# A tuned convolution-and-rational-network kernel: literal biases by rescaling, one engine relieved, head reordered

## The chip, the cores and the metric

The kernel runs on one core of one Trainium2 chip. The metric is the device time of one execution in microseconds (us). The core's engines work side by side and meet through semaphores: TensorE (PE; PEld is its weight load), VectorE (DVE), ScalarE (ACT), GpSimd (POOL) and SyncE (SP), whose queue issues all the DMAs here.

## The reference

First comes a depthwise convolution over 7 steps of the sequence, with a softmax over its taps, for 8 heads of 24 channels each. Its result is the input of a network with a rational function between two products:

```python
w = softmax(weight)                              # (8 heads, 7 taps)
x = causal_conv(x, w).reshape(32768, 192)        # x: (8, 4096, 192)
h = x @ w_in                                     # (192, 2048)
P = a[0] + a[1]*h + a[2]*h**2 + a[3]*h**3
Q = 1.0 + abs(b[0])*abs(h) + abs(b[1])*h**2
out = (P / (Q + 1e-6)) @ w_out                   # (2048, 192)
```

a is drawn as four normal numbers times 0.3, b as two times 2.4. For the default seed b is 0.417 and 1.823.

## The kernel before

**Chunks and units.** The 32768 tokens are cut into 64 chunks of 512 (NCH), the 2048 hidden channels into 8 units of 256 (UPC). So there are 512 units, numbered k = 8c + i. For each chunk, `conv` (task c, two halves, 108 small matmuls) makes the convolution in PSUM; ScalarE casts it (xh, L394 and L397) and VectorE takes the residuals (xl, L404 and L408). For each unit, `gemm1` (g1, 10 matmuls, L417) makes h in one of two PSUM buffers (tile hp). Then come the passes over 128 x 1024 elements below, and `gemm2` (g2, 16 matmuls in two pairs, L426) adds g times the second weights into the one PSUM tile op. At a chunk's end `out_evac` (O, L435) scales it into ob, and SP writes it out.

**The passes of a unit on the fast path** (function `unit`), with K0, K1, K2, BETA, DD columns of the tile cf:

- S (ScalarE, L457): t = square(h + K2). A (ScalarE, L461): A = abs(r_sq h), with a scale from a register.
- B (ScalarE, L464): A = square(A + BETA). L (L471): y = ln(A + DD). Y (L473): y = exp(-y), the reciprocal of the denominator.
- V (VectorE): t = (t + K1) h. m (VectorE): g = (t + K0) y.
- e: A = (A + DD) y. In even units it is one VectorE operation; in odd units (ON_POOL) it is two on GpSimd, q (L483, the sum) and e (L486, the product).
- g (VectorE): g = (A - 2) g. This product by a value near 1 makes up for the error of y.

VectorE's V, m, e and g all come through the helper `stt` and show as L258: V writes t, e writes A, m is g<-t,cf,y and g is g<-A,g.

**The branch.** A fast path and a general path are both in the program. The flag ok, worked out on VectorE from a and b, decides at run time. The general path has a fifth VectorE pass (U) and other ScalarE arguments. Before the change, the condition on b is b0 squared / 8 <= |b1|.

**The weights.** They arrive as 64-bit floats in 16 pieces (8 of w_in, called i, and 8 of w_out, called o, in the order RAW, through 8 buffers) and are made into 32-bit ones during chunk 0, by the steps a, d (ScalarE), m (GpSimd), s, o (VectorE), r (GpSimd), and for w_in h (ScalarE, the upper part wh_t) and l (GpSimd, the lower part wl_t). Chunk 0's products wait for them.

**What sets the order.** `plan` works out one fixed order of all tasks on the engines by a list schedule: each task has an engine, a cost from the table COST (or PREP), dependences and a rank; an engine that comes free takes the ready task of the lowest rank. TensorE's own order is written by hand: g1(k), at i = 4 the next chunk's two convolution halves, then g2(k - 3). Dependences put in for buffers are that g1(k) waits for V, A and S of k - 2, and g2 of a chunk's first unit waits for the O of the chunk before. Each engine then runs its queue in that order and waits where data is late. The head (softmax of the taps, flag, coefficients, first loads) lies ahead of that, and the transfers go out on SP's queue in the order of the code.

Of the kernel before, what the change touches and what calls it, by code (L numbers as in the profile page):

```python
# [166 lines left out]
def kernel(  # L167
# [91 lines left out]

    a = [ab_t[:, i:i + 1] for i in range(6)]  # L260
    nc.scalar.activation(out=cf[:, B0:B0 + 2], in_=ab_t[:, 4:6], func=AF.Abs)
    nc.scalar.activation(out=cf[:, 18:22], in_=ab_t[:, 0:4], func=AF.Abs)
    m0, m1, m2, m3 = (col(18 + i) for i in range(4))
# [293 lines left out]
```

## Time and profile before

| | |
|---|---|
| median of 3 runs | 2833.69 us (2833.64 to 2834.93) |
| profiled execution, time | 2833.45 us |
| profiled execution, span (first to last instruction) | 2831.6 us |
| mean granted TensorE clock | 0.992 of full speed |
| busy PE / PEld / DVE / ACT / POOL | 2701.2 / 2407.0 / 2437.2 / 2757.8 / 1508.8 us |

Busy time is a sum over the span. The end is set by whichever engine others wait for in a stage, so stages are read apart: the head with chunk 0, the steady chunks, the end. Neighbouring operations of one engine overlap by some 0.1 us in their durations, so the distance between starts is what an engine's pace is read from.

### The profile page before, as it was taken

What the parts mean: (1) busy time and instruction counts of PE and PEld (TensorE: products, weight loads), DVE (VectorE), ACT (ScalarE), POOL (GpSimd) and SP (SyncE); (2) the same over time, 40 slices, a digit from 0 to 9 for tenths busy, and PEclk for the clock granted to TensorE, in tenths of its full rate; (3) what the DMA queues carried; (4) which work ended last, traced back from release to release, by engine and by line L of the source; (5) the groups of instructions that cost most, each with busy time, mean ns of one, the idle gap of its engine ahead of it and who ended that gap; (6) DMA issues with size and microseconds to landing.
All of it is one profiled execution on the core that took longest, in us unless ns stands there. A gap on an engine that the chain in (4) does not pass through costs nothing.

```text
span 2831.6 us, 49117 instructions
## 1 busy us (share of the span) xinstructions
PE 2701.2 (95%) x20224; PEld 2407.0 (85%) x20224; DVE 2437.2 (86%) x2061; ACT 2757.8 (97%) x2927; POOL 1508.8 (53%) x560
## 2 busy tenths in 40 slices
PE   5899999999999999999999999999999999999998
PEld 4788888888888888888888888888888888888887
DVE  6888888888888888888888888888888888888887
ACT  6899999999999999999999999999999999999998
POOL 7755555455554555555554545545555555545454
PEclk8999999999999999999999999999999999999999
DMA  4000000000000000000000000000000000000000
GB/s 135 13 23 14 25 19 19 25 19 19 25 16 22 25 13 25 23 14 25 18 19 25 18 19 25 16 22 25 13 25 23 15 25 18 19 25 18 19 12 13
DMA packets 49194, 64.44 MB, mean 23 GB/s; under 512 B 4672, under 2 KB 43840, under 8 KB 48960
## 3 DMA queue, kind: packets, MB, share of 16 engines
q1 hardware_dynamic: 48960, 61.22, 7.6%
q8 instruction: 160, 2.62, 0.4%
q14 instruction: 74, 0.61, 0.1%
HBM read 36.03 MB, written 25.17 MB: 22 GB/s over the span
## 4 chain that ended last, share of the span: by engine, by line
ACT 60%; issue 18%; PE 8%; POOL 8%; DVE 5%; DMA 0%; SPq 0%; DVEq 0%; POOLq 0%
ACT A L464 14%; ACT t L457 13%; ACT A L461 12%; ACT y L471 10%; ACT y L473 6%; PE hp L417 4%; POOL A L486 4%; POOL A L483 3%; PE op L426 2%; DVE g L258 2%; DVE A L258 2%; PE cps L387 2%; ACT xh L397 1%; ACT xh L394 1%; ACT ob L435 1%
## 5 line engine op out<-in xcount | busy, mean ns | idle before, releaser
L483 POOL TENSOR_SCALAR A<-A,cf 128x1024 f32<-128x1024 f32 x256 | 795.6, 3108 | 1257.8 <-ACT y L471 1257.8
L426 PE MATMUL op<-wo_t,g 128*128 128x192 f32 x8192 | 1431.2, 328 | 5.2 <-DVE g L258 4.2
L426 PEld LDWEIGHTS op<-wo_t,g 128*128 128x128 f32 x8192 | 1351.1, 190 | 63.2 <-ACT ob L435 23.9
L417 PE MATMUL hp<-xh,wh_t 128*128 128x512 f32 x2048 | 870.6, 425 | 105.4 <-DVE t L258 90.2
L258 DVE SCALAR_TENSOR_TENSOR g<-A,g 128x1024 f32<-128x1024 f32 x512 | 678.1, 1324 | 267.0 <-POOL A L486 267.0
L258 DVE SCALAR_TENSOR_TENSOR g<-t,cf,y 128x1024 f32<-128x1024 f32 x512 | 763.5, 1491 | 87.4 <-ACT y L473 87.4
L486 POOL TENSOR_TENSOR A<-A,y 128x1024 f32<-128x1024 f32 x256 | 649.9, 2539 | 34.8 <-DVE xh L408 18.7
L258 DVE SCALAR_TENSOR_TENSOR t<-t,cf,hp 128x1024 f32<-128x1024 f32 x512 | 650.7, 1271 | 0.3 <-ACT t L457 0.3
L417 PE MATMUL hp<-xh,wl_t 128*128 128x512 f32 x2048 | 639.5, 394 | 6.2 <-POOL wl_t L364 6.1
L471 ACT ACTIVATE y<-A,cf 128x1024 f32<-128x1024 f32 x512 | 588.8, 1150 | 16.4
L464 ACT ACTIVATE A<-A,cf 128x1024 f32<-128x1024 f32 x512 | 587.6, 1148 | 0.0
L457 ACT ACTIVATE t<-hp,cf 128x1024 f32<-128x1024 f32 x512 | 567.9, 1109 | 0.0
L417 PEld LDWEIGHTS hp<-xh,wh_t 128*128 128x128 f32 x2048 | 388.0, 189 | 207.6 <-DVE t L258 72.9
L473 ACT ACTIVATE y<-y 128x1024 f32<-128x1024 f32 x512 | 539.7, 1054 | 6.3
L461 ACT ACTIVATE A<-hp 128x1024 f32<-128x1024 f32 x512 | 514.9, 1006 | 1.9 <-PE hp L417 1.9
L417 PEld LDWEIGHTS hp<-xh,wl_t 128*128 128x128 f32 x2048 | 387.3, 189 | 96.1 <-POOL wl_t L364 8.9
L417 PE MATMUL hp<-xl,wh_t 128*128 128x512 f32 x1024 | 404.6, 395 | 0.0
L258 DVE SCALAR_TENSOR_TENSOR A<-A,cf,y 128x1024 f32<-128x1024 f32 x256 | 328.4, 1283 | 0.0
L417 PEld LDWEIGHTS hp<-xl,wh_t 128*128 128x128 f32 x1024 | 194.8, 190 | 20.7
L387 PEld LDWEIGHTS cps<-wb_t,xs 128*32 128x32 f32 x6912 | 117.1, 149 | 30.9 <-issue 30.9
L387 PE MATMUL cps<-wb_t,xs 128*32 128x58 f32 (+1 forms) x6912 | 125.1, 229 | 7.9 <-DVE cf L290 7.9
L435 ACT ACTIVATE ob<-op 128x384 f32<-128x384 f32 x128 | 62.3, 488 | 8.8 <-PE op L426 8.8
(46 smaller groups left out, 311.0 us busy)
## 6 DMA issues: line engine op xcount, KB each, us to landing
out<-ob SPq DMA_DIRECT2D x128, 192.0 KB, 2.0
xs<-in_xa SPq DMA_DIRECT2D x64, 324.0 KB, 3.9
xs<-in_xb SPq DMA_DIRECT2D x64, 108.0 KB, 3.7
raw<-in_w_in SPq DMA_DIRECT2D x8, 512.0 KB, 8.6
raw<-in_w_out SPq DMA_DIRECT2D x8, 384.0 KB, 7.5
wb_t<-in_wband SPq DMA_DIRECT2D x1, 174.0 KB, 2.4
mb_t<-in_mband SPq DMA_DIRECT2D x1, 174.0 KB, 2.7
wr_t<-in_wrep SPq DMA_DIRECT2D x1, 21.0 KB, 2.4
```

The lines of the kernel that those rows point to most:

```text
L258: nc.vector.scalar_tensor_tensor(out=out_, in0=a, scalar=s, in1=b, op0=op0, op1=op1)
L387: nc.tensor.matmul(cps[32 * j:32 * j + 32, blk * BW:blk * BW + n], lhsT=xs[:, :, blk, g], rhs=wb_t[:, g, 0:n], start=True, stop=True, tile ...
L417: nc.tensor.matmul(H[k][:, j, :], lhsT=w[:, i, part, j, :], rhs=x, start=(n == 0), stop=(n == 4))
L426: nc.tensor.matmul(O[c][:, t, 0:D], lhsT=G[k][:, j, t * P:t * P + P], rhs=wo_t[:, f, :], start=(f == 0 and t % 2 == 0), stop=(f == FT - 1 ...
L435: nc.scalar.activation(out=ob, in_=o, func=AF.Copy, scale=r_na3)
L457: nc.scalar.activation(out=work_tile(k, "t"), in_=h, func=AF.Square, bias=col(K2))
L461: nc.scalar.activation(out=work_tile(k, "A"), in_=h, func=AF.Abs, scale=r_sq if fast else r_b0)
L464: nc.scalar.activation(out=s["A"], in_=s["A"], func=AF.Square, bias=col(BETA))
L471: nc.scalar.activation(out=y, in_=s["A"], func=AF.Ln, bias=col(DD) if fast else C_Q)
L473: nc.scalar.activation(out=s["y"], in_=s["y"], func=AF.Exp, scale=-1.0)
L483: nc.gpsimd.tensor_scalar(s["A"], s["A"], col(DD), None, ALU.add)
L486: nc.gpsimd.tensor_tensor(out=s["A"], in0=s["A"], in1=s["y"], op=ALU.mult)
```

## The change

The fast path's formulas are rescaled so that the biases of S, B and L become the literal 1: S is square(rt h + 1), A is abs(rA h) with another scale, B is square(A + 1), L is ln(rL A + 1), where rt, rA, rL (and rO for O) are scales in ScalarE registers. VectorE's passes keep their form with new constants: V with c1, m with c0, e with d, and g with d2 = 2d from a tile where the literal 2 stood. All units do e on VectorE; GpSimd's q and e are gone, so GpSimd only prepares weights (and the general path's Q).

The coefficients are no longer worked out in the head. A new VectorE task k (43 operations on 128 x 1, then four register loads on ScalarE) does so behind chunk 0's residuals, and every S and A depends on it. The flag's condition is written anew, with b0 squared <= 3 |b1| and bounds on both, and stands behind the softmax in the code. The first weight piece is loaded ahead of chunk 0's x. The costs and arrival times of `plan` are set anew. The entry of h in the table H is deleted with g and no longer with V.

The diff, cut to its core (the general path's side and the old coefficient code are left out):

```diff
-COST = {"c": 1100, "g1": 2290, "g2": 1300, "xh": 460, "xl": 600, "S": 905, "A": 905, "B": 905, "L": 949, "Y": 958,
-        "V": 1198, "m": 1198, "e": 1200, "g": 1142, "q": 1250, "f": 2500, "O": 357, "U": 1198, "Q": 2500}
+COST = {"c": 950, "g1": 2280, "g2": 1300, "xh": 460, "xl": 600, "S": 905, "A": 905, "B": 905, "L": 949, "Y": 950,
+        "V": 1195, "m": 1196, "e": 1196, "g": 1142, "k": 6000, "O": 357, "U": 1198, "Q": 2500}
...
-ON_POOL = (1, 3, 5, 7)
...
-    arrive, last = 9000, {}
+    arrive, last = 5500, {}
     for n, (which, i) in enumerate(RAW):
-        arrive += 2600 if which == "i" else 2000
+        arrive += (2600 if which == "i" else 2000) + (2200 if n in (1, 3) else 0)
...
-            add(("c", c, half), "PE", COST["c"], deps, 0, 6000 if c == 0 else 0)
+            add(("c", c, half), "PE", COST["c"], deps, 0, 9800 if c == 0 else 0)
...
+    add(("k", 0), "DVE", COST["k"], [("xl", 0, 0), ("xl", 0, 1)], -40)
...
-        add(("S", k), "ACT", COST["S"], [("g1", k)] + old(4, "m"), 8 * k + 1)
-        add(("A", k), "ACT", COST["A"], [("g1", k)] + old(4, "g"), 8 * k)
+        add(("S", k), "ACT", COST["S"], [("g1", k), ("k", 0)] + old(4, "m"), 8 * k + 1)
+        add(("A", k), "ACT", COST["A"], [("g1", k), ("k", 0)] + old(4, "g"), 8 * k)
...
-        if fast and i in ON_POOL:
-            add(("q", k), "POOL", COST["q"], [("L", k)], 8 * k + 5)
-            add(("e", k), "POOL", COST["f"], [("q", k), ("Y", k)], 8 * k + 6)
-        else:
-            add(("e", k), "DVE", COST["e"], [("Y", k)], 8 * k + 6)
+        add(("e", k), "DVE", COST["e"], [("Y", k)], 8 * k + 6)
...
+    load_w(*RAW[0])
     load_x(0)
-    for which, i in RAW[:2]:
+    for which, i in RAW[1:3]:
         load_w(which, i)
     load_x(1)
-    for which, i in RAW[2:NRAW]:
+    for which, i in RAW[3:NRAW]:
         load_w(which, i)
-
...
-    stt(col(K2), a[2], 0.5, col(R3), ALU.mult, ALU.mult)
...
-    stt(col(BETA), col(B0), 0.5, col(RQ), ALU.mult, ALU.mult)
-    stt(col(T0), col(BETA), -1.0, col(BETA), ALU.mult, ALU.mult)
-    ts(col(DD), col(T0), C_Q, None, ALU.add)
...
-    for name, i in (("r_b0", B0), ("r_sq", SQ), ("r_na3", NEG_A3)):
-        reg = nc.scalar.alloc_register(name)
-        nc.scalar.reg_load(reg, col(i)[0:1].bitcast(I32))
-        scales.append(reg)
-    r_b0, r_sq, r_na3 = scales
...
+    stt(less[:, 6:7], b0, 1.0, b0, ALU.mult, ALU.mult)
+    ts(more[:, 6:7], b1, 3.0, None, ALU.mult)
...
+    nc.vector.tensor_tensor(out=less, in0=less, in1=more, op=ALU.is_le)
+    nc.vector.tensor_reduce(out=col(24), in_=less, axis=AX.X, op=ALU.min)
+    nc.vector.tensor_copy(out=ok, in_=col(24))
...
-                nc.scalar.activation(out=ob, in_=o, func=AF.Copy, scale=r_na3)
+                nc.scalar.activation(out=ob, in_=o, func=AF.Copy, scale=K["rO"])
...
+        def coefficients():
...
+            def div(x, y):
+                r, q = spare(), spare()
+                nc.vector.reciprocal(out=r, in_=y)
+                stt(q, r, -1.0, y, ALU.mult, ALU.mult)
+                stt(r, q, 2.0, r, ALU.add, ALU.mult)
+                stt(r, x, 1.0, r, ALU.mult, ALU.mult)
+                return r
+
+            regs = {}
+            if fast:
+                regs["t"] = div(a[3], a[2])
+                ts(regs["t"], regs["t"], 2.0, None, ALU.mult)
+                K["c0"], K["c1"], K["d"], K["d2"], w, x = (spare() for _ in range(6))
+                ts(w, regs["t"], 2.0, None, ALU.mult)
+                inv = div(w, a[2])
+                stt(K["c0"], a[0], 1.0, inv, ALU.mult, ALU.mult)
+                stt(K["c1"], a[1], 1.0, inv, ALU.mult, ALU.mult)
+                ts(K["c1"], K["c1"], -1.0, None, ALU.add)
+                regs["A"] = div(b1, b0)
+                ts(regs["A"], regs["A"], 2.0, None, ALU.mult)
...
+                ts(x, b0, 0.0, 1.0, ALU.mult, ALU.add)
+                regs["L"] = div(x, K["d"])
...
+                regs["O"] = div(w, x)
...
+            for name, x in regs.items():
+                K["r" + name] = nc.scalar.alloc_register(f"r_{name}_{fast}")
+                nc.scalar.reg_load(K["r" + name], x[0:1].bitcast(I32))
...
+            if kind == "k":
+                coefficients()
+            elif kind == "S":
                 if fast:
-                    nc.scalar.activation(out=work_tile(k, "t"), in_=h, func=AF.Square, bias=col(K2))
+                    nc.scalar.activation(out=work_tile(k, "t"), in_=h, func=AF.Square, scale=K["rt"], bias=1.0)
...
             elif kind == "A":
-                nc.scalar.activation(out=work_tile(k, "A"), in_=h, func=AF.Abs, scale=r_sq if fast else r_b0)
+                nc.scalar.activation(out=work_tile(k, "A"), in_=h, func=AF.Abs, scale=K["rA"])
             elif kind == "B":
                 if fast:
-                    nc.scalar.activation(out=s["A"], in_=s["A"], func=AF.Square, bias=col(BETA))
+                    nc.scalar.activation(out=s["A"], in_=s["A"], func=AF.Square, bias=1.0)
...
             elif kind == "L":
-                y = work_tile(k, "y") if fast else s["y"]
-                nc.scalar.activation(out=y, in_=s["A"], func=AF.Ln, bias=col(DD) if fast else C_Q)
+                if fast:
+                    nc.scalar.activation(out=work_tile(k, "y"), in_=s["A"], func=AF.Ln, scale=K["rL"], bias=1.0)
...
             elif kind == "V":
-                stt(s["t"], s["t"], col(K1) if fast else na1, h, ALU.add, ALU.mult)
-                del H[k]
+                stt(s["t"], s["t"], K["c1"], h, ALU.add, ALU.mult)
             elif kind == "m":
                 G[k] = gpool.tile([P, 2, CH], F32, name="g")
-                stt(flat(G[k]), s["t"], col(K0) if fast else na0, s["y"], ALU.add, ALU.mult)
-            elif kind == "q":
-                nc.gpsimd.tensor_scalar(s["A"], s["A"], col(DD), None, ALU.add)
+                stt(flat(G[k]), s["t"], K["c0"], s["y"], ALU.add, ALU.mult)
             elif kind == "e":
-                if fast and k % UPC in ON_POOL:
-                    nc.gpsimd.tensor_tensor(out=s["A"], in0=s["A"], in1=s["y"], op=ALU.mult)
-                else:
-                    stt(s["A"], s["A"], col(DD) if fast else C_Q, s["y"], ALU.add, ALU.mult)
+                stt(s["A"], s["A"], K["d"] if fast else C_Q, s["y"], ALU.add, ALU.mult)
             elif kind == "g":
-                stt(flat(G[k]), s["A"], 2.0, flat(G[k]), ALU.subtract, ALU.mult)
-                del st[k]
+                stt(flat(G[k]), s["A"], K["d2"] if fast else 2.0, flat(G[k]), ALU.subtract, ALU.mult)
+                del st[k], H[k]
```

## Rows read from the trace of the kernel before

**Rows 1.** Engines' busy time (share of the span, instructions), and the chain of work that ended last, shares by engine.

```profile
PE 2701.2 (95%) x20224; PEld 2407.0 (85%) x20224; DVE 2437.2 (86%) x2061; ACT 2757.8 (97%) x2927; POOL 1508.8 (53%) x560
...
ACT 60%; issue 18%; PE 8%; POOL 8%; DVE 5%; DMA 0%; SPq 0%; DVEq 0%; POOLq 0%
```

**Rows 2.** The table by stretches: from:to, length, busy us of PE, PEld, DVE, ACT, POOL with counts, granted clock, DMA share, GB/s.

```profile
0.00:44.00 44.00, 15.97 (x138) 10.87 (x138) 27.98 (x68) 24.38 (x40) 30.62 (x28) 0.83 0.72 201
...
500.00:931.00 431.00, 419.02 (x3162) 374.19 (x3161) 374.96 (x311) 427.08 (x451) 225.64 (x80) 1.00 0.07 21
```

**Rows 3.** The first evacuations of chunk 0 and of chunk 62 in ScalarE's timeline (start, us, what), with, between them, the group of A passes from 114 to 2786.6 us.

```profile
114.23 0.49 ACT L435 ACTIVATE ob<-op 128x384 f32<-128x384 f32 x1
...
L461 ACT ACTIVATE A<-hp 128x1024 f32<-128x1024 f32 x496 | 498.8, 1006 | 0.0
...
2786.53 0.48 ACT L435 ACTIVATE ob<-op 128x384 f32<-128x384 f32 x1
```

**Rows 4.** Who waited for whom from 114 to 2786 us: us in total, times, longest.

```profile
PEld hp L417 <- DVE t L258: 54.9, 61, 0.9
PEld hp L417 <- issue: 53.0, 61, 1.4
PEld op L426 <- ACT ob L435: 23.6, 62, 1.2
```

**Rows 5.** ScalarE's passes, grouped from 114 to 2786.6 us (count | busy us, mean ns | idle us before); A is in group 3.

```profile
L471 ACT ACTIVATE y<-A,cf 128x1024 f32<-128x1024 f32 x496 | 570.5, 1150 | 16.1
L464 ACT ACTIVATE A<-A,cf 128x1024 f32<-128x1024 f32 x496 | 569.3, 1148 | 0.0
L457 ACT ACTIVATE t<-hp,cf 128x1024 f32<-128x1024 f32 x496 | 550.2, 1109 | 0.0
L473 ACT ACTIVATE y<-y 128x1024 f32<-128x1024 f32 x496 | 522.9, 1054 | 6.1
```

**Rows 6.** ScalarE's timeline in the steady part: S, B, L and the next A.

```profile
1397.04 1.10 ACT L457 ACTIVATE t<-hp,cf 128x1024 f32<-128x1024 f32 x1
1398.04 1.14 ACT L464 ACTIVATE A<-A,cf 128x1024 f32<-128x1024 f32 x1
1399.21 1.15 ACT L471 ACTIVATE y<-A,cf 128x1024 f32<-128x1024 f32 x1
1400.27 1.00 ACT L461 ACTIVATE A<-hp 128x1024 f32<-128x1024 f32 x1
```

**Rows 7.** TensorE's weight loads in the timeline: one unit with a convolution, then one without.

```profile
1411.66 0.19 PEld L417 LDWEIGHTS hp<-xh,wh_t 128*128 128x128 f32 x1
...
1414.22 1.80 PEld L387 LDWEIGHTS cps<-wb_t,xs 128*32 128x32 f32 x108 [0.36 <-issue]
...
1418.62 0.19 PEld L417 LDWEIGHTS hp<-xh,wh_t 128*128 128x128 f32 x1
...
1429.27 0.19 PEld L417 LDWEIGHTS hp<-xh,wh_t 128*128 128x128 f32 x1
...
1434.15 0.19 PEld L417 LDWEIGHTS hp<-xh,wh_t 128*128 128x128 f32 x1
```

**Rows 8.** VectorE's timeline in the steady part: an m beside GpSimd's q (which runs from 1395.38 for 3.87 us), then g, m, e, V, g.

```profile
1397.18 1.42 DVE L258 SCALAR_TENSOR_TENSOR g<-t,cf,y 128x1024 f32<-128x1024 f32 x1 [0.65 <-ACT y L473]
...
1401.74 1.23 DVE L258 SCALAR_TENSOR_TENSOR g<-A,g 128x1024 f32<-128x1024 f32 x1 [1.96 <-POOL A L486]
1402.88 1.28 DVE L258 SCALAR_TENSOR_TENSOR g<-t,cf,y 128x1024 f32<-128x1024 f32 x1
1404.08 1.28 DVE L258 SCALAR_TENSOR_TENSOR A<-A,cf,y 128x1024 f32<-128x1024 f32 x1
1405.28 1.27 DVE L258 SCALAR_TENSOR_TENSOR t<-t,cf,hp 128x1024 f32<-128x1024 f32 x1
1406.47 1.25 DVE L258 SCALAR_TENSOR_TENSOR g<-A,g 128x1024 f32<-128x1024 f32 x1
```

**Rows 9.** VectorE's timeline from a chunk's first residual to the g behind the last.

```profile
65.60 0.88 DVE L408 TENSOR_TENSOR xh<-cps,xh 64x290 fp32r<-64x290 f32 x2
...
67.11 1.59 DVE L258 SCALAR_TENSOR_TENSOR g<-A,g 128x1024 f32<-128x1024 f32 x1
```

**Rows 10.** VectorE's m, grouped from 500 to 931 us.

```profile
L258 DVE SCALAR_TENSOR_TENSOR g<-t,cf,y 128x1024 f32<-128x1024 f32 x80 | 119.8, 1497 | 14.0 <-ACT y L473 14.0
```

**Rows 11.** The table by stretches, the first 104 us (columns as in group 2).

```profile
0.00:104.00 104.00, 58.27 (x401) 46.73 (x402) 74.87 (x110) 68.71 (x96) 83.02 (x54) 0.80 0.33 92
```

**Rows 12.** GpSimd's q and e, grouped from 0 to 92.7 us.

```profile
L483 POOL TENSOR_SCALAR A<-A,cf 128x1024 f32<-128x1024 f32 x3 | 10.2, 3400 | 0.0
...
L486 POOL TENSOR_TENSOR A<-A,y 128x1024 f32<-128x1024 f32 x3 | 7.1, 2356 | 0.1
```

**Rows 13.** VectorE's timeline in the head: two of the coefficient operations, then the second weight piece's s step.

```profile
7.10 0.15 DVE L255 TENSOR_SCALAR cf<-cf 128x1 f32<-128x1 f32 x1
7.29 0.22 DVE L258 SCALAR_TENSOR_TENSOR cf<-cf,ab_t 128x1 f32<-128x1 f32 x1
...
17.73 1.50 DVE L352 TENSOR_SCALAR tr<-ad 128x512 uint32<-128x512 uint32 x1 [2.90 <-POOL ad L346]
```

**Rows 14.** TensorE's timeline in the head: the first product.

```profile
16.95 0.80 PE L417 MATMUL hp<-xh,wh_t 128*128 128x512 f32 x1 [6.20 <-ACT wh_t L362]
```

**Rows 15.** VectorE's timeline at the end: the last g.

```profile
2821.72 1.23 DVE L258 SCALAR_TENSOR_TENSOR g<-A,g 128x1024 f32<-128x1024 f32 x1 [2.24 <-POOL A L486]
```

More of the change, by code (lines that the diff above doesn't have):

```diff
@@ L217 @@
     sm = const.tile([P, NG], F32, name="sm")
-    cf = const.tile([P, 32], F32, name="cf")
+    cf = const.tile([P, 64], F32, name="cf")
     ok = const.tile([P, 1], I32, name="ok")
@@ L258, in stt @@
         nc.vector.scalar_tensor_tensor(out=out_, in0=a, scalar=s, in1=b, op0=op0, op1=op1)
[L260 to L263, printed above, removed]
-    ts(col(T0), m3, 2.0 ** -40, None, ALU.is_ge)
-    stt(col(T1), m2, 1.0 / 16.0, m3, ALU.mult, ALU.is_le)
-    stt(col(T0), col(T0), 1.0, col(T1), ALU.mult, ALU.mult)
@@ L448, in work_tile, with spare @@
             return t
-        na0, na1, na2, na3 = (col(NEG + i) for i in range(4))
+        K = {}
+        def coefficients():
+            def spare():
+                K["n"] = K.get("n", 24) + 1
+                return col(K["n"])
+            def div(x, y):
[17 more added lines that the diff above has]
+                ts(regs["A"], regs["A"], 2.0, None, ALU.mult)
+                ts(w, regs["A"], 2.0 * C_Q, None, ALU.mult)
+                d = div(w, b0)
+                ts(K["d"], d, -1.0, None, ALU.add)
+                ts(K["d2"], K["d"], 2.0, None, ALU.mult)
+                ts(x, b0, 0.0, 1.0, ALU.mult, ALU.add)
+                regs["L"] = div(x, K["d"])
+                ts(w, regs["A"], 2.0, None, ALU.mult)
+                beta2 = div(b0, w)
+                stt(w, K["d"], 1.0, beta2, ALU.mult, ALU.mult)
+                stt(w, w, 1.0, K["d"], ALU.mult, ALU.mult)
+                stt(x, w, -1.0, inv, ALU.mult, ALU.mult)
+                ts(w, b0, 0.0, 1.0, ALU.mult, ALU.add)
+                regs["O"] = div(w, x)
+            else:
+                K["c0"], K["c1"], K["c2"], regs["t"] = (spare() for _ in range(4))
+                for x, y in zip((K["c0"], K["c1"], K["c2"], regs["t"]), a):
+                    ts(x, y, -1.0, None, ALU.mult)
+                regs["A"] = b0
+                root, rec = spare(), spare()
+                ts(root, b1, 1e-30, None, ALU.max)
+                nc.scalar.activation(out=root, in_=root, func=AF.Ln)
+                nc.scalar.activation(out=root, in_=root, func=AF.Exp, scale=0.5)
+                nc.vector.reciprocal(out=rec, in_=root)
+                stt(root, rec, b1, root, ALU.mult, ALU.add)
+                ts(root, root, 0.5, None, ALU.mult)
+                regs["B"] = root
+            for name, x in regs.items():
+                K["r" + name] = nc.scalar.alloc_register(f"r_{name}_{fast}")
+                nc.scalar.reg_load(K["r" + name], x[0:1].bitcast(I32))
@@ L469, in unit @@
             elif kind == "L":
-                y = work_tile(k, "y") if fast else s["y"]
-                nc.scalar.activation(out=y, in_=s["A"], func=AF.Ln, bias=col(DD) if fast else C_Q)
+                if fast:
+                    nc.scalar.activation(out=work_tile(k, "y"), in_=s["A"], func=AF.Ln, scale=K["rL"], bias=1.0)
+                else:
+                    nc.scalar.activation(out=s["y"], in_=s["A"], func=AF.Ln, bias=C_Q)
             elif kind == "Y":
```

59 lines of the change are left out of this document (19 added, 40 removed).

## The prediction

> **What bounds the kernel now.** I read the page first for the engines' shares and the chain that ended last: ScalarE is busy 97% of the span, TensorE 95%, VectorE 86%, and the chain runs 60% over ScalarE [rows 1]. Such shares mix stages, so next comes the table by stretches: in the middle ScalarE is busy 427.1 of 431 us, at a granted TensorE clock of 1.00, the 2.4 GHz level [rows 2]. Then the evacuations of the output, one pair per chunk: chunk 0's first is at 114.23 us, chunk 62's at 2786.53, with 62 x 8 units of ScalarE passes between [rows 3]. A chunk takes (2786.53 - 114.23) / 62 = 43.10 us. So the time is a head of 114.2, 62 chunks of 43.10 and a rest of 2831.6 - 2786.5 = 45.1. The steady chunk is ScalarE's: it hardly idles, while TensorE's weight loads wait for VectorE's t pass (V) (54.9 + 53.0, the latter named issue) and for the output's evacuation (23.6) [rows 4], in all (54.9 + 53.0 + 23.6) / 62 = 2.1 us a chunk.
>
> **ScalarE's passes.** Three of five take a bias from the tile cf: S 1109 ns, B 1148, L 1150; two take none: A, from PSUM, 1006, Y, from SBUF, 1054 [rows 5]. The change makes these three biases the literal 1. No row has a pass with a literal bias other than zero, so its cost lies between the bias-free rows and the tile rows. I take the bias-free ones, as Y already runs with a literal scale of -1 and A with a register scale at no visible price. S is then like A, B and L like Y: (1109 - 1006) + (1148 - 1054) + (1150 - 1054) = 103 + 94 + 96 = 293 ns a unit, 2.34 us a chunk. ScalarE's chunk falls from 43.10 to 40.76, if its order stays. It can fall further: L starts 1.17 us after the B that it needs, where other neighbours start 1.00 and 1.06 apart [rows 6]; eight such joints are worth about 1 us, if the new order parts them. Bounds for ScalarE: 39.8 to 43.10.
>
> The Trainium skill has a price for this, in "ScalarE: Activation LUTs", section "What ACT_TABLE_LOAD costs": a pass with literal scale and bias has the smaller fixed cost, and each per-partition operand adds about 93 ns. By it, ScalarE's chunk would be 43.10 - 24 x 0.093 = 40.87, an estimate; the rows' 94 to 103 ns agree and go into the sum.
>
> **What is late next: TensorE.** Where nothing holds it, one unit's first weight load follows the last one's by 1434.15 - 1429.27 = 4.88 us; the unit with a convolution takes 1418.62 - 1411.66 = 6.96, of which 0.36 is a gap named issue in front of the convolution [rows 7]. A chunk is 7 x 4.88 + 6.96 = 41.12 us, more than ScalarE's 40.76. So the gain per chunk is capped near 43.10 - 41.12 = 1.98, and not 2.34.
>
> **VectorE takes four more passes.** The product e of the odd units leaves GpSimd and its q disappears; VectorE does e for all 8 units, and g gets a tile scalar (d2) for the literal 2. Neighbours start 1.20 us apart after m and after e, 1.19 after V, 1.14 after a g with the literal [rows 8]; g with a tile scalar is taken at e's 1.20. A unit is 4.79, eight are 38.3, and the two residual steps of the next chunk add 67.11 - 65.60 = 1.51 [rows 9]: 39.8 us a chunk. This hides under TensorE's 41.12 with 1.3 us to spare. The other bound: m averages 1497 ns where it runs 1.28 alone [rows 8, 10]; if that stretch stayed on m, a unit would be 5.01 and a chunk 41.6. I take the short rows, since the 1.42 us m in group 8 ran beside a GpSimd pass and the 1.28 ones did not. What is queued behind VectorE is V, which frees the PSUM buffer that TensorE wants two units later.
>
> **The steady chunk.** Floor 41.12; of the 2.1 us that TensorE waits now, some stay, since ScalarE at 40.76 and VectorE at 39.8 are both close behind and only two PSUM buffers lie between. With none left the chunk is 41.1, with all 43.1. I take 0.3 (nearer to none: the waits arise because ScalarE is slower than TensorE, which ends): 41.4, a saving of 62 x 1.7 = 105 us. The waits of VectorE for GpSimd's product (1.96 us ahead of one g, [rows 8]) go too, and are worth nothing by themselves, as VectorE isn't the bound.
>
> **The head.** GpSimd is busy 83.0 of the first 104 us [rows 11]; until the last l step, which ends at 92.7, q and e take 10.2 + 7.1 = 17.3 of it [rows 12], between the steps of the weight preparation that chunk 0 waits for. Against it stands the new step k: the coefficients, until now interleaved in VectorE's idle start, become 43 small operations behind chunk 0's residuals. Neighbours of that kind start 0.19 apart (7.10 to 7.29 us) [rows 13], so 8.2 us. Behind k on VectorE wait the s and o steps of the second weight piece, which begin at 17.73 now [rows 13]; with k from about 13 to 21 they are 3.5 late. Behind its four register loads on ScalarE wait chunk 0's S and A, which need them, and the a, d and h steps of later pieces, whose room is GpSimd's backlog. Four more e on VectorE (4.8) count by half, as VectorE idles in the head. Gain 17.3 - 3.5 - 2.4 = 11. Bounds: 17 if all of GpSimd's time comes back, a loss of 13 if nothing does and k and the four e count in full. On SP's queue the first weight piece now goes ahead of chunk 0's x, which comes later by one issue of about 0.5 us and by 512 KB at the head's mean rate of 201 GB/s [rows 2], 2.6 us: the convolution may start up to 3 us later. I cost this at nothing, since the first product waits until 16.95 for the weights, 6.2 us of it idle [rows 14]; if that cover is gone, it costs those 3. The first part of the coefficient work that stays ahead of the branch is smaller than now and costs nothing.
>
> **The rest.** At the end the last g waits 2.24 us for GpSimd's product [rows 15]; that wait goes, and the last chunk gets 1.7 shorter: 45.1 - 3.9 = 41.1.
>
> **Sum.** 103.2 + 62 x 41.4 + 41.1 = 2711.1 us of span. The profiled execution took 2833.45 against its span of 2831.6, so 1.9 lie around it; it is 0.2 under the median of the runs. Forecast: 2713 us.
>
> **The rivals.**
> (a) The waits stay. ScalarE and VectorE alternate in a fixed order, and bursts (the casts after a convolution, the evacuations) make V late, so that TensorE keeps losing over a microsecond a chunk, or m stays stretched. For it: three engines within 1.3 us of one another. Against: a unit's first product is through 1414.22 - 0.36 - 1411.66 = 2.2 us after it begins [rows 7], and its buffer is wanted two units, 9.8 us, after that beginning, which leaves over 7 us for A, S and V. At 42.3 a chunk: 103.2 + 2622.6 + 42 + 1.9 = 2770.
> (b) TensorE is quicker than I read: the 0.36 gap before the convolution goes, since ScalarE no longer delays anything. A chunk of 40.76 gives 103.2 + 2527.1 + 40.5 + 1.9 = 2673.
> (c) The change doesn't do what it says: the literal 1 costs as much as the tile did. ScalarE's chunk stays 43.1, only head and end gain: 103.2 + 2672.2 + 42.8 + 1.9 = 2820.
> (d) Slower: VectorE becomes the bound. With 32 passes a chunk and 1.51 of residuals, it passes 43.10 when passes follow one another by 1.30 us on average. If the three passes that read two SBUF tiles kept the 1497 ns of today's m (1.42 apart) and V its 1.20, a chunk would be 8 x 5.46 + 1.51 = 45.2: 103.2 + 2802 + 47 + 1.9 = 2954. For it: that mean. Against: it is seen beside GpSimd, which is idle after the head.
> The Trainium skill bears on this in "SBUF — State Buffer", section "SBUF: two separate sides": a VectorE instruction with two SBUF inputs and a GpSimd one that reads SBUF lock each other out of a shared port pair. By that rule the stretch ends with GpSimd's passes; the trace agrees as far as the m of 1.42 and 1.28 us go.
> (e) The narrower condition fails for the inputs and the general path runs: five VectorE passes a unit, 8 x 5 x 1.20 + 1.51 = 49.5 a chunk, some 3220 us. The drawn b has b0 squared over |b1| of 0.095, against an allowed 3.
>
> **How the numbers follow.** Forecast (chunks of 41.1 to 41.9, 2690 to 2745): 0.60. (a) 0.17, (b) 0.11, (c) 0.04, (d) 0.04, (e) 0.02, anything else 0.02. For 8 in 10, the range reaches into (b) and (a): 2668 to 2775; the head's bounds (6 us less to 24 more) lie within. This kernel can be told from no change by about 0.2%, 6 us. Faster: the forecast, (a), (b) and three quarters of (c) with the rest, 0.92; the same 0.02; slower, with (d) and (e), 0.06.
>
> **What would show it.** Right: S near 1006 ns, B and L near 1054; TensorE's weight loads following without waits for most of a chunk, evacuations 41 to 42 us apart; V, m, e and g all 1.2 us apart; GpSimd idle after some 85 us; chunk 0's evacuation near 103. Wrong: S, B or L unchanged; VectorE busy throughout with TensorE waiting for it over 1 us a chunk; chunk 0 later than 114, with VectorE's run of tiny operations in its chain.

## The result, and the profile of the changed kernel

The changed kernel takes 2704.05 us (median of 4 runs, 2703.7 to 2705.01) against 2833.80 before in the same comparison: a ratio of 0.9542, 95% interval 0.9525 to 0.9558. It is faster by 4.6%; the forecast was 2713 with a range of 2668 to 2775. The profiled execution took 2705.01 us, with a span of 2703.2 and a mean granted clock of 0.992, the same as before.

The page first, engines' busy time and shares of the chain that ended last, to be laid beside [rows 1]:

```profile
PE 2647.6 (98%) x20224; PEld 2412.1 (89%) x20224; DVE 2592.2 (96%) x2339; ACT 2604.8 (96%) x2924; POOL 65.3 (2%) x48
...
PE 96%; DVE 1%; POOL 1%; ACT 1%; issue 1%; DMA 0%; SPq 0%; POOLq 0%; DVEq 0%
```

The chain has gone over from ScalarE (60% before) to TensorE (96%). ScalarE is still 96% busy, so its share of busy time alone would not tell that it no longer bounds anything. The steady stretch, from the table by stretches (columns as in [rows 2]):

```profile
500.00:931.00 431.00, 431.00 (x3268) 393.71 (x3268) 418.42 (x367) 423.06 (x472) 0.00 (x0) 1.00 0.07 21
```

TensorE is busy all 431 us, and GpSimd does nothing. ScalarE's first evacuation of chunk 0 and of chunk 62, as in [rows 3]:

```profile
110.60 0.49 ACT L396 ACTIVATE ob<-op 128x384 f32<-128x384 f32 x1 [1.07 <-PE op L387]
...
2659.57 0.49 ACT L396 ACTIVATE ob<-op 128x384 f32<-128x384 f32 x1 [0.50 <-PE op L387]
```

A chunk is (2659.57 - 110.60) / 62 = 41.11 us instead of 43.10. Of the 128.4 us that the span lost, 123.3 came from the 62 steady chunks, 1.99 each. Head and rest, which were 114.2 + 45.1 = 159.3, are 110.6 + 43.6 = 154.2: another 5.1, of which 3.6 in the head and 1.5 in the rest.

Who waited for whom from 97 to 2660 us, the three largest entries (us in total, times, longest):

```profile
DVE g L249 <- ACT y L493: 73.1, 62, 1.8
ACT ob L396 <- PE op L387: 31.4, 63, 1.1
PEld cps L348 <- issue: 21.8, 62, 0.4
```

TensorE's waits for VectorE's t pass and for the evacuation [rows 4] are gone from the list. What is left of TensorE's own is the 0.35 us in front of each convolution. VectorE and ScalarE now wait once a chunk, for ScalarE and for TensorE: that is what the slack of engines that don't bound looks like. ScalarE's passes, grouped from 500 to 1793 us (count | busy us, mean ns | idle us before), against [rows 5]:

```profile
L489 ACT ACTIVATE y<-A 128x1024 f32<-128x1024 f32 x253 | 268.1, 1060 | 8.0
L482 ACT ACTIVATE A<-A 128x1024 f32<-128x1024 f32 x252 | 267.2, 1060 | 0.0
L493 ACT ACTIVATE y<-y 128x1024 f32<-128x1024 f32 x252 | 264.4, 1049 | 0.0
L475 ACT ACTIVATE t<-hp 128x1024 f32<-128x1024 f32 x252 | 256.8, 1019 | 0.0
L479 ACT ACTIVATE A<-hp 128x1024 f32<-128x1024 f32 x252 | 253.6, 1006 | 0.0
```

S fell from 1109 to 1019 ns, B from 1148 to 1060, L from 1150 to 1060: 90 + 88 + 90 = 268 ns a unit. A is as it was, and Y nearly so. VectorE, grouped from 500 to 931 us:

```profile
L249 DVE SCALAR_TENSOR_TENSOR t<-t,cf,hp 128x1024 f32<-128x1024 f32 x85 | 108.2, 1273 | 0.0
L249 DVE SCALAR_TENSOR_TENSOR g<-t,cf,y 128x1024 f32<-128x1024 f32 x84 | 107.3, 1278 | 11.7 <-ACT y L493 11.7
L249 DVE SCALAR_TENSOR_TENSOR A<-A,cf,y 128x1024 f32<-128x1024 f32 x84 | 107.3, 1278 | 0.0
L249 DVE SCALAR_TENSOR_TENSOR g<-A,cf,g 128x1024 f32<-128x1024 f32 x84 | 107.3, 1277 | 0.0
```

The m that averaged 1497 ns [rows 10] takes 1278. TensorE's pace is seen in the block loads of the output product, one unit and the next, in its timeline:

```profile
1403.63 2.69 PEld L387 LDWEIGHTS op<-wo_t,g 128*128 128x128 f32 x16
...
1408.51 2.69 PEld L387 LDWEIGHTS op<-wo_t,g 128*128 128x128 f32 x16
```

They are 4.88 us apart, what [rows 7] have for units that nothing holds; at this pace, with 6.95 us for the unit with the convolution, a chunk takes its 41.11.

### The profile page after: what moved, and what is told of

It is laid out like the page before. It is cut to its first block, busy times and chain, and to the rows that moved or that the text cites. A ratio compares the mean times of both kernels' runs of the same rounds, so it can differ in the third digit from the quotient of the medians.

```text
span 2703.2 us, 48126 instructions
## 1 busy us (share of the span) xinstructions
PE 2647.6 (98%) x20224; PEld 2412.1 (89%) x20224; DVE 2592.2 (96%) x2339; ACT 2604.8 (96%) x2924; POOL 65.3 (2%) x48
## 4 chain that ended last, share of the span: by engine, by line
PE 96%; DVE 1%; POOL 1%; ACT 1%; issue 1%; DMA 0%; SPq 0%; POOLq 0%; DVEq 0%
PE op L387 49%; PE hp L378 42%; PE cps L348 4%; POOL ad L307 0%; DVE g L249 0%; POOL tr L321 0%; DMA xs<-in_xb 0%; POOL wo_t L321 0%; DVE A L249 0%; DVE cf L249 0%; ACT A L479 0%; DVE t L249 0%; ACT A L482 0%; ACT y L493 0%; ACT t L475 0%
## 5 line engine op out<-in xcount | busy, mean ns | idle before, releaser
L249 DVE SCALAR_TENSOR_TENSOR g<-t,cf,y 128x1024 f32<-128x1024 f32 x512 | 655.4, 1280 | 74.3 <-ACT y L493 74.3
L249 DVE SCALAR_TENSOR_TENSOR A<-A,cf,y 128x1024 f32<-128x1024 f32 x512 | 658.9, 1287 | 0.0
L249 DVE SCALAR_TENSOR_TENSOR g<-A,cf,g 128x1024 f32<-128x1024 f32 x512 | 654.9, 1279 | 0.0
L489 ACT ACTIVATE y<-A 128x1024 f32<-128x1024 f32 x512 | 542.5, 1060 | 16.0
L482 ACT ACTIVATE A<-A 128x1024 f32<-128x1024 f32 x512 | 542.9, 1060 | 0.0
L475 ACT ACTIVATE t<-hp 128x1024 f32<-128x1024 f32 x512 | 521.7, 1019 | 0.0
L479 ACT ACTIVATE A<-hp 128x1024 f32<-128x1024 f32 x512 | 515.3, 1006 | 0.8 <-PE hp L378 0.8
L369 DVE TENSOR_TENSOR xh<-cps,xh 64x290 fp32r<-64x290 f32 (+1 forms) x128 | 54.0, 422 | 3.7
L358 ACT CAST xh<-cps 64x290 fp32r<-64x290 f32 (+1 forms) x128 | 46.2, 361 | 3.5 <-PE cps L348 2.7
```

The costliest lines, as they stand in the source:

```text
L249: nc.vector.scalar_tensor_tensor(out=out_, in0=a, scalar=s, in1=b, op0=op0, op1=op1)
L358: nc.scalar.copy(out=xh[p], in_=CP[c, half][p])
L369: nc.vector.tensor_tensor(out=xh[q], in0=cps[p], in1=xh[p].bitcast(F32), op=ALU.subtract)
L475: nc.scalar.activation(out=work_tile(k, "t"), in_=h, func=AF.Square, scale=K["rt"], bias=1.0)
L479: nc.scalar.activation(out=work_tile(k, "A"), in_=h, func=AF.Abs, scale=K["rA"])
L482: nc.scalar.activation(out=s["A"], in_=s["A"], func=AF.Square, bias=1.0)
```

## The experiments

Theory: ScalarE's and TensorE's paces are two floors under the chunk. The literal biases take ScalarE's floor below TensorE's, and the chunk ends there; the move of e keeps VectorE and GpSimd from making waits. Rivals: the move of e does it, or the new order of the passes, or the bound is still ScalarE's. The table collects what the runs gave, from the same rows in each (chunk 0's first evacuation, the chunk, head and rest together, the median, and the ratio to the kernel before measured beside it, with its interval).

| run | first evacuation | chunk | head + rest | median us | ratio |
|---|---|---|---|---|---|
| before | 114.23 | 43.10 | 159.3 | 2833.80 | |
| changed | 110.60 | 41.11 | 154.2 | 2704.05 | 0.954 (0.9525 to 0.9558) |
| e1, one tile bias | 110.23 | 41.23 | 152.9 | 2712.02 | 0.957 (0.9556 to 0.9588) |
| e11, two tile biases | 110.27 | 41.96 | 153.5 | 2757.05 | 0.973 (0.9714 to 0.9744) |
| e2, three tile biases | 109.15 | 42.68 | 154.6 | 2801.06 | 0.988 (0.9867 to 0.9900) |
| e3, e back on GpSimd | 119.80 | 41.42 | 163.7 | 2733.73 | 0.965 (0.9633 to 0.9665) |
| e4, before with e on VectorE | 107.05 | 43.09 | 150.5 | 2825.14 | 0.997 (0.9961 to 0.9982) |
| e9, before with a new cost | 114.94 | 42.67 | 160.7 | 2808.17 | 0.991 (0.9893 to 0.9923) |
| e10, changed with old costs | 109.42 | 41.12 | 151.9 | 2702.52 | 0.953 (0.9521 to 0.9547) |
| e5, short product | 109.76 | 40.48 | 152.1 | 2663.60 | 0.940 (0.9384 to 0.9415) |
| e6, coefficients early | 102.56 | 41.11 | 145.3 | 2696.59 | 0.952 (0.9499 to 0.9531) |
| e7, x first | 110.53 | 41.11 | 154.1 | 2704.76 | 0.954 (0.9525 to 0.9556) |
| e8, both | 105.86 | 41.11 | 149.3 | 2699.76 | 0.953 (0.9509 to 0.9541) |

**The biases: one, two, three of them as tiles again.** A column is set to 1.0 once and given as bias; values don't change.

```diff
+    nc.vector.memset(col(63), 1.0)
...
-                    nc.scalar.activation(out=work_tile(k, "y"), in_=s["A"], func=AF.Ln, scale=K["rL"], bias=1.0)
+                    nc.scalar.activation(out=work_tile(k, "y"), in_=s["A"], func=AF.Ln, scale=K["rL"], bias=col(63))
```

One (L), expected:

> The changed kernel with one bias (that of L) read from a tile column that holds 1. Theory (TensorE sets the steady chunk at 41.1 us; ScalarE, at 8 units of 4.81 plus 2.0 for casts and evacuations = 40.5, is hidden): L grows by 90 ns, ScalarE needs 40.5 + 0.72 = 41.2, just at TensorE's floor, so chunks of 41.1 to 41.3 and 2704 to 2715 us. Rival (each tile bias costs its 90 ns in full, ScalarE still sets the chunk): chunk 41.83, about 2749 us.

Two (L and B, the line of B changed in the same way), expected:

> The changed kernel with the tile of ones as bias in B and L, S with the literal. Theory, the longer of ScalarE's 40.48 + 0.72 per tile bias (8 passes of 0.09) and TensorE's 41.11: one bias gave 41.23, three 42.68, so two give 40.48 + 1.44 = 41.92, a span of 109.5 + 62 x 41.92 + 44 = 2752.5, time 2754. Rival, the engines begin to wait for one another before the crossing, the rise bends over several tenths: chunk above 42.1, 2766 or more.

Three (S as well), expected:

> The changed kernel with all three biases (S, B, L) read from a tile column that holds 1; everything else as changed. Theory (the literal biases give the gain): the three passes go back to about 1109, 1148 and 1150 ns, ScalarE needs 40.5 + 2.15 = 42.65 a chunk and sets it, 2704 + 62 x 1.5 = 2797 us and a little more. Rival (the gain came from GpSimd's leaving the steady chunk): chunk stays near 41.1 and the time within 10 us of 2704.

The chunk goes 41.11, 41.23, 41.96, 42.68. The last two steps are 0.73 and 0.72, which is 8 passes of 0.09; the first is 0.12. That is one floor under a slope: ScalarE's chunk is 40.48 (from e5, below) + 0.72 per tile bias, and TensorE's 41.11 covers the first. e11 came out 3 us above its forecast, most of it as 0.04 us a chunk, and e1, next to the crossing, has 41.23 where 40.48 + 0.72 = 41.20: the engines hardly wait for one another there. With three tile biases the waits of TensorE are back (same view, 97 to 2640 us):

```profile
PEld op L388 <- ACT ob L397: 58.6, 59, 1.0
PEld hp L379 <- DVE t L249: 37.2, 181, 0.2
PE op L388 <- ACT ob L397: 33.4, 59, 0.6
```

So the literal biases make most of the gain: 97 us of the 130 hang on them, with everything else of the change in place.

**The move of e alone, and all but the move.** The kernel before with no unit's e on GpSimd:

```diff
-ON_POOL = (1, 3, 5, 7)
+ON_POOL = ()
```

> The kernel before with one change: e of all units on VectorE, q gone, biases still from the tile. Theory (ScalarE sets its chunk): chunk stays 43.1; the time falls by the head's and the end's share alone, 2 to 17 us, so 2816 to 2832. If the first chunk's evacuation moves up by more than 10 us, GpSimd's passes were on the head's path, as I forecast; if by less than 4, they were not. Rival (relief of GpSimd gives the chunk's gain): chunk below 42, under 2770 us.

The chunk stays at 43.09: GpSimd's relief and a shorter m are worth nothing there while ScalarE bounds. Head and rest lose 8.9 us (7.2 of them in the head, between the two marks that the expectation set for GpSimd's passes, 4 and 10), the time 8.1. The changed kernel with q and e of the odd units put back on GpSimd, planner's costs and tasks included:

```diff
+ON_POOL = (1, 3, 5, 7)
...
+            elif kind == "q":
+                nc.gpsimd.tensor_scalar(s["A"], s["A"], K["d"], None, ALU.add)
+            elif kind == "e" and fast and k % UPC in ON_POOL:
+                nc.gpsimd.tensor_tensor(out=s["A"], in0=s["A"], in1=s["y"], op=ALU.mult)
```

> The changed kernel with q and e of the odd units back on GpSimd (as before the change), literal biases kept. Theory (TensorE's floor hides VectorE, the move is worth nothing in the steady chunk): chunk 41.1, the time 2704 plus what the head loses (up to 15 us) plus 2 at the end, 2706 to 2722. Rival (VectorE's waits for GpSimd's product and its stretched passes return into the loop through the PSUM buffers): chunk 41.8 to 43.1, 2745 to 2830 us.

It came out between the two expectations, at 2733.7. Head and rest are 9.5 us longer, about what e4 says. But the chunk is 41.42 as well, 0.31 more. TensorE's weight loads in the timeline show where, once a chunk:

```profile
1420.55 0.19 PEld L383 LDWEIGHTS hp<-xh,wh_t 128*128 128x128 f32 x1 [0.31 <-issue]
```

Its total in the waits from 97 to 2680 us, with VectorE's largest:

```profile
DVE g L254 <- POOL A L509: 197.6, 187, 3.4
...
PEld hp L383 <- issue: 19.5, 61, 0.3
```

And VectorE's m, grouped from 500 to 931 us:

```profile
L254 DVE SCALAR_TENSOR_TENSOR g<-t,cf,y 128x1024 f32<-128x1024 f32 x83 | 124.1, 1495 | 7.4 <-ACT y L498 7.4
```

61 waits of 0.3 are 19.5 us, the whole of 62 x 0.31. The wait stands ahead of the product that needs its PSUM buffer back. "issue" names no releaser, but the timelines of VectorE (m and the V behind it) and of GpSimd (its product) show it:

```profile
1416.32 2.92 DVE L254 SCALAR_TENSOR_TENSOR g<-t,cf,y 128x1024 f32<-128x1024 f32 x1
1419.16 1.27 DVE L254 SCALAR_TENSOR_TENSOR t<-t,cf,hp 128x1024 f32<-128x1024 f32 x1
```

```profile
1415.74 2.42 POOL L509 TENSOR_TENSOR A<-A,y 128x1024 f32<-128x1024 f32 x1 [0.31 <-DVE xh L374]
```

The m starts while GpSimd's product has 1415.74 + 2.42 - 1416.32 = 1.84 us to go, and takes 2.92 instead of 1.28. V, which frees the buffer, therefore ends at 1420.43, and TensorE's load follows 0.12 us later. It is so in all 61 waits: an m of 2.9 us, the V behind it, TensorE 0.12 behind that. The mean of 1495 ns comes from this one m in each chunk (11 of the 83; the others take 1.27 to 1.29). So the same edit has another price once the bound has moved: before, the move was worth nothing in the steady chunk and 8 us in all; behind the literal biases it is worth 0.31 us a chunk and 30 us in all.

**The order of ScalarE's passes.** e2 has all of ScalarE's old costs back, yet its chunk is 42.68, not e4's 43.09. Its timeline differs in one thing: in three of eight units the kernel before has Y right behind the L that it reads. ScalarE's timeline, e4 (L, Y, A, S) and then e9 (L, A, Y, S):

```profile
1414.35 1.15 ACT L471 ACTIVATE y<-A,cf 128x1024 f32<-128x1024 f32 x1
1415.53 1.06 ACT L473 ACTIVATE y<-y 128x1024 f32<-128x1024 f32 x1
1416.50 1.01 ACT L461 ACTIVATE A<-hp 128x1024 f32<-128x1024 f32 x1
1417.40 1.11 ACT L457 ACTIVATE t<-hp,cf 128x1024 f32<-128x1024 f32 x1
```

```profile
1414.30 1.15 ACT L471 ACTIVATE y<-A,cf 128x1024 f32<-128x1024 f32 x1
1415.36 1.00 ACT L461 ACTIVATE A<-hp 128x1024 f32<-128x1024 f32 x1
1416.26 1.04 ACT L473 ACTIVATE y<-y 128x1024 f32<-128x1024 f32 x1
1417.21 1.11 ACT L457 ACTIVATE t<-hp,cf 128x1024 f32<-128x1024 f32 x1
```

From L to the next S it is 3.05 us against 2.91. The order is chosen by the planner from its costs, and the change sets several of them anew. e9 is the kernel before with one of these numbers, the cost of a convolution's half:

```diff
-COST = {"c": 1100, "g1": 2290, "g2": 1300, "xh": 460, "xl": 600, "S": 905, "A": 905, "B": 905, "L": 949, "Y": 958,
+COST = {"c": 950, "g1": 2290, "g2": 1300, "xh": 460, "xl": 600, "S": 905, "A": 905, "B": 905, "L": 949, "Y": 958,
```

> The kernel before with one number changed, the planner's cost of a convolution's half, 1100 to 950 as in the change. By the planner this moves 183 of the 200 units whose Y stands right behind the L that it reads (three of eight in each chunk) to the order L, A, Y; nothing else in the kernel changes, and the biases stay tiles. Theory, order counts where ScalarE is the bound: a unit ordered S, B, L, Y, A takes 1417.40 - 1412.18 = 5.22 us in the trace of the kernel before with e on VectorE, one ordered S, B, L, A, Y 5.08, so 183 x 0.14 = 26 us less: about 2808, with a chunk of 42.68. Rival, the difference of 0.41 us between that kernel's chunk and the chunk of the changed kernel with three tile biases is due to something else (register scales, the dropped residual cost, another order of VectorE): 2834, chunk 43.1. A result between says that both have a part.

2808.2 with a chunk of 42.67: the theory to the microsecond. By the traces, Y stands right behind its L in 196 units of the kernel before and in 10 of e9, and the order of VectorE's large passes is the same in both. The converse, the changed kernel with the three old costs:

```diff
-COST = {"c": 950, "g1": 2280, "g2": 1300, "xh": 460, "xl": 600, "S": 905, "A": 905, "B": 905, "L": 949, "Y": 950,
+COST = {"c": 1100, "g1": 2290, "g2": 1300, "xh": 460, "xl": 600, "S": 905, "A": 905, "B": 905, "L": 949, "Y": 958,
```

> The changed kernel with the planner's three old costs (convolution half 1100, product 2290, Y 958), which puts three of eight units in each chunk back to S, B, L, Y, A. Theory, TensorE is the bound now: ScalarE's own chunk rises from 40.48 to 40.48 + 3 x 0.14 = 40.90, still under TensorE's 41.11, so the time stays at 2704 to 2708. Rival, ScalarE's order is paid even here, by waits of TensorE: chunk 41.11 + 0.42, 2730.

The chunk is 41.12, and the time 2702.5, 1.5 us less than the changed kernel. So the order alone was worth 26 us and is worth nothing now: ScalarE's 0.42 us a chunk go under TensorE's floor.

**TensorE is the bound now.** The first product of each unit with 8 matmuls in place of 10:

```diff
-            terms = [(wh_t, 0, xhA), (wh_t, 0, xlA), (wh_t, 1, xB), (wl_t, 0, xhA), (wl_t, 1, xB)]
+            terms = [(wh_t, 0, xhA), (wh_t, 0, xlA), (wh_t, 1, xB), (wl_t, 0, xhA)]
```

> The changed kernel with one of the five terms of the first product left out (the low weights times the B part of x), so 8 instead of 10 matmuls a unit; the output lacks that small term. Theory (TensorE's 41.11 us is the chunk, ScalarE is next at 8 x 4.81 + 2.0 = 40.5): TensorE falls to 41.1 - 8 x 0.456 = 37.5, and the chunk stops at ScalarE's 40.3 to 40.6, so 2704 - 62 x 0.6 = 2667, 2655 to 2675 us. Rival (the loop over two PSUM buffers sets the pace, each unit's A, S and V, not TensorE's throughput): TensorE's shorter product shortens the loop by all of it, chunk under 40, below 2640. If chunks stay at 41.1, TensorE was not the bound.

2663.6, and the chunk falls to 40.48 only. The steady stretch:

```profile
500.00:931.00 431.00, 420.05 (x3231) 365.25 (x3230) 424.24 (x374) 427.90 (x481) 0.00 (x0) 1.00 0.08 22
```

The waits from 97 to 2640 us:

```profile
PEld hp L378 <- DVE t L249: 109.4, 313, 0.6
PEld op L387 <- ACT ob L396: 55.8, 63, 1.0
```

ScalarE is back at 427.9 of 431, next to the 427.1 of the kernel before, and TensorE waits again. So TensorE was the bound, and ScalarE's floor lies 0.63 us beneath it.

**The head.** e6 issues the coefficients' operations at the start of the fast path (in its trace they run from 6.53 to 15.92 us, the last of them among the first weight steps) and leaves only the four register loads in k; e7 loads chunk 0's x ahead of the first weight piece, as before; e8 does both. The two edits:

```diff
-        "V": 1195, "m": 1196, "e": 1196, "g": 1142, "k": 6000, "O": 357, "U": 1198, "Q": 2500}
+        "V": 1195, "m": 1196, "e": 1196, "g": 1142, "k": 300, "O": 357, "U": 1198, "Q": 2500}
...
-            for name, x in regs.items():
+            K["regs"] = regs
+
+        def load_scales():
+            for name, x in K["regs"].items():
...
-                coefficients()
+                load_scales()
...
+        coefficients()
```

```diff
-    load_w(*RAW[0])
...
-    for which, i in RAW[1:3]:
+    for which, i in RAW[:2]:
...
-    for which, i in RAW[3:NRAW]:
+    for which, i in RAW[2:NRAW]:
```

> The changed kernel with the 43 small coefficient operations of k issued on VectorE at the start of the fast path, ahead of all planned tasks; only the four register loads stay in k (its cost 300 ns). Theory (k is on the head's chain, with ScalarE blocked 8.5 us behind its register loads): the block from 14.4 to 22.9 us goes; VectorE idles 4.6 us of the time into which it moves, so 4 to 8 us are won: 2696 to 2700 us. Rival (the head is VectorE's and GpSimd's backlog over the whole first chunk, into which the 8.5 us go anyway): within 2 us of 2704.

> The changed kernel with the order of the first transfers as before the change (chunk 0's x, then the weight pieces). Theory (the convolution's wait for x, at 10.2 instead of 7.8 us, is on the head's chain, since k follows chunk 0's residuals): k starts 2 us earlier, 2 us won, 2701 to 2703 us. Rival (hidden, as I forecast): 2703 to 2706 us.

> Both together: coefficients at the start of the fast path, and x first. Theory: with k out of the way the order of the transfers decides little, VectorE is busy with the coefficients until about 15 us either way; 2696 to 2700 us, as with the coefficients early alone. Rival: the gains add up, 2694 to 2697 us.

e6 takes 2696.6, with the first evacuation 8.0 us earlier. What it took away is seen in the head of the changed kernel. First TensorE's first product, VectorE's first and last entries of k, then ScalarE and the second unit's product (timeline, wait in brackets):

```profile
14.32 0.80 PE L378 MATMUL hp<-xh,wh_t 128*128 128x512 f32 x1 [1.24 <-ACT wh_t L323]
14.38 0.15 DVE L420 RECIPROCAL cf<-ab_t 128x1 f32<-128x1 f32 x1
...
22.38 0.55 DVE L249 SCALAR_TENSOR_TENSOR cf<-cf 128x1 f32<-128x1 f32 x3
23.31 0.66 ACT L305 ACTIVATE ad<-raw 128x512 int32<-128x512 uint32 x1 [8.46 <-DVE tr L313]
...
29.32 0.80 PE L378 MATMUL hp<-xh,wh_t 128*128 128x512 f32 x1 [10.70 <-ACT wh_t L323]
```

ScalarE stands still for 8.46 us. What it starts with then is no S or A but a weight step that needs no coefficient: it stood behind the register loads, which wait for k. (The entry names VectorE's s step as the releaser. In e6 the same weight step starts ahead of that s step, at 16.29 against 16.62, and 0.37 us behind the last coefficient; here it is 0.38.) In e6 that step starts at 16.29 and the second unit's product at 20.73 (ScalarE and TensorE, timeline):

```profile
16.29 0.67 ACT L305 ACTIVATE ad<-raw 128x512 int32<-128x512 uint32 x1 [1.95 <-DVE cf L249]
...
20.73 0.80 PE L378 MATMUL hp<-xh,wh_t 128*128 128x512 f32 x1 [3.67 <-ACT wh_t L323]
```

VectorE's own queue is held up too. GpSimd's m step of the second piece in the changed kernel, and the s step on VectorE that takes its result:

```profile
15.59 1.49 POOL L307 TENSOR_SCALAR ad<-ad 128x512 f32<-128x512 f32 x1
...
22.84 0.42 DVE L313 TENSOR_SCALAR tr<-ad 128x512 uint32<-128x512 uint32 x1
```

The data is there at 17.08, and s starts 5.8 us later, behind k. e6 takes both hold-ups away at once, so how its 8 us share between ScalarE's register loads and VectorE's k is not shown.

The order of the first transfers makes no difference in the changed kernel (e7). The convolution starts at 7.02 us there instead of 10.19, but k not earlier (15.21 against 14.38), as the steps of the now later first weight piece lie ahead of the residuals on VectorE; so e7's theory failed and its rival held. With the coefficients early, x first is 3.2 us slower (e8 against e6): the time is still in the range that I expected for e8, but its reason, that the order decides little, is not borne out. In e8 ScalarE's first weight step starts 1.9 us later than in e6 (10.05 against 8.13) and the second unit's product 2.3 later (23.07 against 20.73). In e7 the first weight step is 1.5 us later than in the changed kernel, but the step behind the register loads only 0.4 (23.74 against 23.31): k's stall covered the rest. e6 is the fastest of the kernels that compute the whole reference, 7.5 us under the changed one.

TensorE runs part of the head at its 1.2 GHz level in all these kernels: the granted clock of the first 110 us is 0.81 before, 0.83 in the changed kernel, 0.84 in e4 and e6, 0.80 in e3 and 0.81 in e8 (1.00 is the 2.4 GHz level). What of the differences between heads is the clock's was not separated.

## Why the prediction came out right, step by step

**The bound and its next.** Right. ScalarE bounded the steady chunk before, and TensorE's 41.12, added up from the unwaited stretches of [rows 7], is the chunk after to 0.01 us. The term that was mis-sized is the 0.3 us of waits that I let stay: none stayed, so the chunk gave 1.99 and not 1.7, 123 us and not 105. Head and rest erred the other way, by 10 us, so that the total of 2713 is closer to 2704 than its terms are; that is luck.

**The literal bias.** The mechanism is right, and the price a little too high: 268 ns a unit against 293. I took the bias-free rows as the price, and passes with a literal 1 measure 1019 and 1060 where A and Y have 1006 and 1054 [rows 5] (they run other functions, so the remainder need not be the bias's). The page of the Trainium skill, "ScalarE: Activation LUTs", section "What ACT_TABLE_LOAD costs", has 93 ns per operand; these runs have 88 to 90. Since TensorE's floor cut ScalarE's gain off, the 25 ns a unit cost nothing.

**The order.** The step "if its order stays" was wrong without harm. I looked at the joint from B to L, which the new order doesn't part (L still starts 1.09 us behind B, at 1397.60 and 1398.69). The one from L to Y was parted, by a planner cost that I had read as bookkeeping, and it is worth 26 us by itself. With the literals it is hidden, so the forecast didn't notice. ScalarE's floor of 40.48 rather than my 40.76 is made of both: 43.10 - 0.42 - 8 x 0.268 = 40.54.

**VectorE.** Right: passes follow one another by 1.19 to 1.20 us and the long m was GpSimd's doing, since it is 1278 ns with GpSimd idle and 1495 in e3. Its mean of 1497 [rows 10] was no stretch of every m, as I took it for the other bound: of the 80, ten take 2.9 us, ten 1.4 and sixty 1.27 to 1.29. Rival (d) had no ground behind the head. In the head both engines still work, and its rows (VectorE's and GpSimd's timelines) show how the stretch comes about. GpSimd:

```profile
63.33 1.92 POOL L321 TENSOR_TENSOR wo_t<-wo_t,ad 128x384 int32<-128x384 int32 x1 [0.96 <-DVE wo_t L317]
...
73.13 2.18 POOL L321 TENSOR_TENSOR tr<-tr,ad 128x512 int32<-128x512 int32 x1 [2.41 <-DVE tr L317]
...
85.54 2.17 POOL L321 TENSOR_TENSOR tr<-tr,ad 128x512 int32<-128x512 int32 x1 [2.25 <-DVE tr L317]
```

VectorE:

```profile
64.30 2.03 DVE L249 SCALAR_TENSOR_TENSOR A<-A,cf,y 128x1024 f32<-128x1024 f32 x1
...
74.09 1.27 DVE L249 SCALAR_TENSOR_TENSOR t<-t,cf,hp 128x1024 f32<-128x1024 f32 x1
...
86.50 2.28 DVE L249 SCALAR_TENSOR_TENSOR A<-A,cf,y 128x1024 f32<-128x1024 f32 x1
```

The e at 64.30 starts while GpSimd's pass has 63.33 + 1.92 - 64.30 = 0.95 us to go, and takes 0.75 longer than 1.28; the e at 86.50 finds 1.21 us to go and takes 1.00 longer. V at 74.09, which reads one of its inputs from PSUM, takes its 1.27 beside a GpSimd pass. The Trainium skill's rule in "SBUF — State Buffer", section "SBUF: two separate sides", says that of such a pair the one that starts later waits out the other's instruction; these rows agree to 0.2 us, and so does e3's m (1.84 us to go, 1.64 longer). All three stand beside a GpSimd pass with two inputs. The m of 1.42 us, which the prediction counts as agreeing, does not fit: q, with one input, had 1395.38 + 3.87 - 1397.18 = 2.07 us to go [rows 8], and that m took only 0.14 longer than 1.28.

**The move of e.** Hidden by itself, as I costed it, and e4 shows it. What I didn't say is what it prevents: with it undone TensorE waits 0.31 us a chunk (e3).

**The head.** Here the sizes were off: of the 11 us forecast, 3.6 came. GpSimd's relief is worth 7.2 us of the head in the old kernel and 9.2 in the changed one (e4, e3), not 17.3 less 2.4. k costs 8 where it stands (e6), not 3.5: it begins at 14.38 and not at 13, the s step behind it starts 5.1 us later than before (22.84 against 17.73), and ScalarE's steps behind the register loads I named and priced at nothing. The transfers' order cost nothing, as forecast. Why GpSimd's 17 shrink to 7 or 9 was not tried by itself. From 44 to 110 us VectorE is busy 61.7 of 66 us and GpSimd 37.9 (table by stretches):

```profile
44.00:110.00 66.00, 48.67 (x314) 41.58 (x315) 61.69 (x58) 51.67 (x64) 37.85 (x24) 0.83 0.07 19
```

GpSimd's passes above wait for VectorE's weight steps, 0.96 to 2.41 us each, and VectorE's e are stretched. So I take it that the head's bound moved to VectorE; this is argued from the rows and not shown.

**The rest.** Of 3.9 us, 1.5 came. The wait for GpSimd's product is gone, and the last g ends 33.5 us behind chunk 62's evacuation instead of 36.4. But TensorE was then still in its last two products, which it ran in one go (TensorE's and VectorE's timelines):

```profile
2689.45 7.15 PE L387 MATMUL op<-wo_t,g 128*128 128x192 f32 x32 [1.94 <-DVE g L249]
...
2691.82 1.28 DVE L249 SCALAR_TENSOR_TENSOR g<-A,cf,g 128x1024 f32<-128x1024 f32 x1
```

It ends 3.5 us behind the last g; before, it needed 2.9. In these 7.15 us, which come after a wait of 1.94, the granted clock was 0.76, part of it at the 1.2 GHz level; in the last product of the kernel before it was 1.00. From the last evacuation to the end it takes 0.9 us longer as well (6.2 against 5.3). I had costed neither.

**The rivals.** (a) fell with the waits gone; (b) fell, as the gap in front of the convolution stands at 21.8 us over 62 chunks; (c) fell with the pass times; (d) and (e) fell with VectorE's 1.2 us pace and its four passes a unit.

## What to carry to other kernels

Work out the pace of every engine for the steady stage from stretches in which it waits for nothing; a gain on the bounding engine is cut off at the next pace, and edits that are worth nothing in the steady chunk before (the move of e) or much before (the order) change price when the bound moves. When a pass on the bounding engine reads the result of the one directly before it, put another between them. Before work is moved behind a dependency in the head, go through the queue of each engine that gets a wait by it, register loads included, and price everything that stands behind it.
